# A fused Fourier filter and MLP on one core: the second tile's layer-norm statistics move to ScalarE, the first fifth of W1 is loaded in half rows, the second fifth ahead of x2, and the order is written anew

## The chip, the core and the metric

The kernel runs on one core of a Trainium2 chip. The metric is the device time of a run in microseconds (us). A core has five engines that run side by side, each with its own in-order list of instructions: TensorE (PE; its weight loads are listed as PEld), VectorE (DVE), ScalarE (ACT), GpSimd (POOL) and the sync engine (SP), which here issues most of the DMAs. They meet only at semaphores. A tile in this text is one of 16 groups of 128 rows of x; x0 and x1 are the loads of the first two, x2 is the load of tiles 2 and 3 together.

## The reference

The input x has 2048 rows of 640. Its normalized form goes through two branches, which are added to x:

```python
xn = _layernorm(x, axis=-1)                       # (x - mean) / sqrt(var + 1e-5)
X  = rfft2(xn, axes=(-2, -1)) * (w_r + 1j * w_i)  # branch A: a filter in the Fourier domain
a  = irfft2(X, s=(2048, 640)).astype(bfloat16)
h  = gelu(xn @ w1 + b1)                           # branch B: 640 -> 1536 -> 640
return x + a + (h @ w2 + b2)
```

x, the weights and the result are bfloat16.

## The kernel before

**The stages.** The 16 tiles are normalized (mean and variance over 640 columns, reciprocal root, then subtract and multiply). The normalized tile is needed in two forms: transposed, in `xnT`, for the first MLP product, and as it is, for the Fourier stages. Tiles 0 to 3 are transposed by TensorE against an identity into PSUM and copied out; tiles 4 to 15 are transposed by DMA. The Fourier branch folds the columns of each pair of tiles (lines 722 and 726), transforms over rows with a table (`gtab`), over columns (`etab`), mixes the rest (`mtab`), multiplies by the filter (line 837), and goes back by `ntab`, a DMA transpose, `getab` and `htab`. The MLP multiplies `W1` with `xnT`, applies the Gelu with the bias (line 770) into `gT`, and multiplies `gT` with `W2`. The last stage adds everything and stores it (lines 948 and 951).

**The head.** For each tile VectorE takes two `bn_stats` (line 666) over 320 columns and one `bn_aggr` (668). A third, constant set of statistics is arranged so that the aggregate's variance already holds the 1e-5. GpSimd then raises the variance to the power -0.5 (670), and VectorE subtracts and multiplies (691). Tile 0 is normalized in two pieces, 256 and 384 columns, so that its first two transposes can start early. The five 128-column blocks of tiles 0 and 1 are transposed in two lots, two and three (710), and copied out by ScalarE and VectorE (716).

**The first product.** `W1` comes in five loads, one for each 128 rows of its 640 (the fifths); each is 128 partitions by 1536 columns. The first block of the product (tiles 0 and 1, `BLOCKS[0]`) makes 12 groups of 128 outputs, and for the first two fifths treats tile 0 and tile 1 apart (128-column products, 48 of them), for the other three together (256 columns). Line 592 writes these loads, line 585 those of x.

**What sets the order.** All engines' lists are written out by hand as numbers in `ORDER` (line 158); a number is the place at which the operation was recorded. The class `Sched` lays these lists out with a model of costs, which chooses PSUM slots and the semaphore waits; it doesn't change the order of a list. On the sync queue x0, x1, the first fifth, x2, the second, third, fifth and fourth fifths go first, then more of x, the table `gtab`, and the rest. A product waits only for the fifth of `W1` that it reads. 38 products on zeros (`idle`, line 571) run on TensorE before there is data.

**Activation tables.** ScalarE evaluates its functions from a table set. A load instruction brings a set in; the kernel places one at the head for the Gelu (line 595), whose set serves the copies too. Where a function isn't in the set that is loaded, the build places a load right ahead of it.

Of the kernel before, what the change touches and what calls it, by code (L numbers as in the profile page):

```python
# [8 lines left out]
F32 = dt.float32  # L9
ACT = mybir.ActivationFunctionType  # L10
# [3 lines left out]
D = 640  # L14
# [109 lines left out]
class Pool:  # L124
# [34 lines left out]
    "sp": """8 13 14 17 15 16 19 18 21 22 20 27 30 23 26 28 153 155 166 168 32 31 35 46 48 37 179 181 192 194 38 39  # L159
41 34 44 33 29 52 49 40 205 219 221 207 43 42 50 45 51 47 36 54 508 506 505 507 529 531 530 532 554 553 53 555  # L160
556 578 577 580 579 597 642 606 623 633 669 659 678 741 695 750 732 715 766 705 775 782 789""",
    "pe": """7 117 55 119 278 260 122 233 251 242 124 269 234 270 243 252 261 281 254 236 235 279 253 263 272 245 264 273 237 282 275 138
# [8 lines left out]
713 776 777 764 770 778 771 779 772 773 780 783 784 785 786 787""",  # L171
    "act": """12 9 118 56 123 139 258 142 276 259 277 267 250 268 249 292 319 240 241 295 135 313 134 136 322 316 310 307 151 298 301 289
# [3 lines left out]
767 670 609 645 644 680 681 717 753""",  # L176
    "dve": """0 58 57 59 61 62 63 115 116 121 120 66 65 125 67 70 69 137 71 127 126 140 128 130 131 129 144 143 74 76 73 77
# [6 lines left out]
781 788""",  # L184
    "pool": """10 11 3 1 2 60 5 64 6 68 72 79 86 93 4 100 107 25 114 24 589 687 615 625 651 707 661 697 724 743 635 599
759 734 768 671""",
}

# [19 lines left out]
ROW_NS = {256: 26, 384: 22, 512: 27, 640: 33, 642: 70, 768: 37, 1024: 47, 1280: 56, 1600: 68, 2560: 103, 3072: 122, 4096: 160, 10272: 750, "acc": 152}  # L208
# [7 lines left out]
class Sched:  # L216
# [38 lines left out]
    def schedule(self):  # L255
# [31 lines left out]
        while left:  # L287
# [178 lines left out]
def bass_parallel_sum__spectral_gfnet__dense_activation_gelu__prompt_kernel(  # L466
# [21 lines left out]
    with ExitStack() as es:  # L488
        def sb(name, shape, dtype=BF):
            return es.enter_context(nc.sbuf_tensor(name, shape, dtype))  # L490
# [23 lines left out]
        rstd = sb("rstd", [128, 16], F32)  # L514
        W1 = sb("W1", [128, 5 * F])
# [49 lines left out]
        K.op([("pool", 0.1)], 94, lambda e, _: e.memset(stats[:, :, 14:15], D * 1e-5), writes=[B_eps])  # L565
        K.op([("pool", 0.1)], 100, lambda e, _: e.memset(mhalf[:], -0.5), writes=[B_mh])
# [12 lines left out]
        B_w1s = [Buf(f"w1_{j}") for j in range(5)]  # L579
        B_g, B_e, B_m, B_n, B_ge, B_h, B_w2 = [Buf(x) for x in ("g", "e", "m", "n", "i", "h", "w2")]  # L580
# [14 lines left out]
        K.op([("act", 1.3)], 420, lambda e, _: e.preload_act_table(ACT.Gelu_apprx_tanh), writes=[Buf("table")])  # L595
# [63 lines left out]
        mv_ops, st_op = [], {}  # L659
        for c0, n in [(c, 1) for c in range(4)] + [(c, 2) for c in range(4, 16, 2)]:  # L660
            pr = 100 - c0 / 2
            B_mv, B_r = Buf(f"mv{c0}"), Buf(f"r{c0}")
            for c in range(c0, c0 + n):
                B_st = Buf(f"st{c}")
                for h in range(2):
                    st_op[c] = K.op([("dve", 0.393)], pr, lambda e, _, c=c, h=h: e.bn_stats(stats[:, c, 6 * h:6 * h + 6], view(X, c * D + H2 * h, [[1, H2]])),  # L666
                         reads=[B_x[c]], writes=[B_st], gate=mv_ops[:1])
                mv_ops.append(K.op([("dve", 0.119)], pr, lambda e, _, c=c: e.bn_aggr(mv[:, c, :], stats[:, c, :]), reads=[B_st, B_eps], writes=[B_mv]))  # L668
            a, b = c0, c0 + n
            K.op([("pool", 0.65)], 500, lambda e, _, a=a, b=b: e.tensor_tensor(out=rstd[:, a:b], in0=mv[:, a:b, 1], in1=mhalf[:, a:b], op=ALU.pow),  # L670
                 reads=[B_mv, B_mh], writes=[B_r] + B_rs[a:b])

        for pair in range(8):
# [10 lines left out]
            for n in range(2):  # L684
# [3 lines left out]
                cuts = (0, 256, D) if not c else (0, D)  # L688
                B_xs = [Buf(f"xn_{c}") for _ in cuts[2:]] + [B_xn]
                for d0, d1, bx in zip(cuts, cuts[1:], B_xs):  # L690
                    o = K.op([("dve", 0.066 + (d1 - d0) / 1980.0)], pr, lambda e, _, c=c, n=n, xnv=xnv, d0=d0, d1=d1: e.tensor_scalar(  # L691
                        out=xnv(n, d0, [[1, d1 - d0]]), in0=view(X, c * D + d0, [[1, d1 - d0]]), scalar1=mv[:, c, 0:1], scalar2=rstd[:, c:c + 1], op0=ALU.subtract, op1=ALU.mult),
                        reads=[B_x[c], B_rs[c]], writes=[xn, bx])
                    norm_ops.append(o)
                if not c:
                    st_op[1].gate += [o] * G1
# [7 lines left out]
                for j0, j1, engs in ((0, 2, ["act"]), (2, 5, ["dve"])) if c < 2 else ((0, 5, ["dve", "act"]),):  # L704
# [8 lines left out]
                    if not c + j0:  # L713
                        tp.deps.remove(norm_ops[1])
# [30 lines left out]
        for bi, (c0, nt) in enumerate(BLOCKS):  # L745
            for fc in range(NFC):
# [4 lines left out]
                if bi:  # L751
                    hps, at, part_ = Buf(f"hps{c0}_{fc}", psum, 1, ZONE["hps"]), 0, []
                    for js in ((0, 1, 2), (3, 4)):
                        part_ = [pe([("128", len(js) * mm_us(128 * nt))], pr + 0.01 * len(part_), lambda c0=c0, nt=nt, fc=fc, hps=hps, js=js: [
                            (psb(hps.slot, [[1, 128 * nt]]), view(W1, F * j + 128 * fc, [[1, 128]]), xnT[:, c0:c0 + nt, j, :], j == 0, j == 4) for j in js],
                            reads=B_w1s + B_xnT[c0:c0 + nt], writes=[hps], gate=part_)]
                        l1_ops += part_
                        l1_of.setdefault(bi, []).extend(part_)
                else:
                    at = 256 * (fc % 2)  # L760
                    if not at:
                        hps, part_ = Buf(f"hps0_{fc}", psum, 1, ANY), []
                        for j in range(5):
                            for t0, t1 in ((0, 1), (1, 2)) if j < LONE else ((0, 2),):
                                part_.append(pe([("128", 2 * mm_us(128 * (t1 - t0)))], pr + 8 - j - 2 * t0, lambda fc=fc, hps=hps, j=j, t0=t0, t1=t1: [
                                    (psb(hps.slot, [[1, 128 * (t1 - t0)]], 256 * h + 128 * t0), view(W1, F * j + 128 * (fc + h), [[1, 128]]), xnT[:, t0:t1, j, :], j == t0 == h == 0, j == 4) for h in range(2)],
                                    reads=[B_w1s[j]] + [B_xnL[t][j] for t in range(t0, t1)], writes=[hps], gate=part_[:1]))
# [37 lines left out]
        for P in range(4):  # L805
# [28 lines left out]
            for pair, Y, TB, Z in zip(two, Ys, TBs, Zs):  # L834
# [5 lines left out]
                for r, op in enumerate((ALU.subtract, ALU.add)):  # L840
                    K.op([("dve", dve_us(2 * KP, 2))], pr, lambda e, _, TB=TB, Z=Z, r=r, op=op: e.tensor_tensor(
                        out=view(Zb, Z.slot * 4 * KP + r * KP, [[2 * KP, 2], [1, KP]]), in0=tv(TB, 0, r), in1=tv(TB, 1, r), op=op), reads=[TB], writes=[Z])
# [32 lines left out]
        for gi, (c0, n) in enumerate(GROUPS):  # L875
# [20 lines left out]
            for i in range(n):  # L896
# [9 lines left out]
                else:  # L906
                    ki = [b for b in range(16) if b not in HOME].index(c)
                    free = norm_ops[:2 * ki + 3]
# [82 lines left out]
```

## Time and profile before

| | |
|---|---|
| median of 3 runs | 148.41 us (148.24 to 148.72) |
| span of the profiled execution, first to last instruction | 146.2 us |
| profiled execution's own time | not given beside its span; 2.2 us lie between that span and the median |
| TensorE, VectorE, ScalarE, GpSimd busy | 140.4, 110.9, 81.1, 23.7 us |
| granted TensorE clock | 1.000 |
| HBM read, written | 13.54 MB, 2.62 MB |

A line of the profile gives start, length, engine, source line, operation, the tiles it writes and reads, and in brackets the time the engine stood idle before it and what released it. Groups give the busy time, the mean of one in ns, and the idle time before them. L546 is the helper through which all products are recorded, L557 and L558 the copies by ScalarE and VectorE, L541 the loads; there one goes by the tiles. W stands for `W1` and `W2`, T for the buffer that holds the normalized tiles.

### The profile page before, as it was taken

Reading aid. Unit: us, or ns where it says so; the run is one execution under the profiler, and the core shown is the slowest. Engines: PE = TensorE matmul, PEld = TensorE weight load, DVE = VectorE, ACT = ScalarE, POOL = GpSimd, SP = SyncE. Lnnn points to the kernel's source line nnn. Section 1 sums busy time; section 2 is a strip of 40 time slices with the busy share of each in tenths; the row PEclk is TensorE's granted clock in tenths of the full one; section 3 lists DMA queues with packets and bytes.
Section 4 is the critical chain, followed back from the end, with each engine's and each line's share of the span. In section 5 each row is a group of like instructions: output and inputs, shape, how many; then the busy total and the mean of one; then the engine's idle time right before and its main releaser. Section 6 shows DMA issues by size and latency. Waiting matters only on the chain.

```text
span 146.2 us, 4076 instructions
## 1 busy us (share of the span) xinstructions
PE 140.4 (96%) x1702; PEld 91.3 (62%) x1720; DVE 110.9 (76%) x233; ACT 81.1 (55%) x145; POOL 23.7 (16%) x40
## 2 busy tenths in 40 slices
PE   7999999999999999999999999999999999999993
PEld 7788998988455464457554645554446766556572
DVE  1799999999953459799877967982203998998982
ACT  3208999999989769763555633225476655201000
POOL 2330401304200009220200040000063700000000
DMA  4999998998999676968446844462569885103234
GB/s 105 328 394 354 319 164 197 203 175 229 241 238 160 162 195 137 242 126 167 89 92 128 56 95 89 46 142 56 91 129 225 178 188 180 45 4 137 90 135 135
DMA packets 30842, 23.63 MB, mean 162 GB/s; under 512 B 20457, under 2 KB 26857, under 8 KB 30697
## 3 DMA queue, kind: packets, MB, share of 16 engines
q1 hardware_dynamic: 28432, 17.81, 52.6%
q0 software_dynamic: 2368, 5.57, 17.6%
q8 instruction: 13, 0.21, 0.6%
q14 instruction: 5, 0.03, 0.1%
q10 hardware_dynamic: 24, 0.00, 0.0%
HBM read 13.54 MB, written 2.62 MB: 111 GB/s over the span
## 4 chain that ended last, share of the span: by engine, by line
PE 92%; DMA 4%; issue 1%; SPq 1%; DVE 0%
PE ps L546 91%; DMA W<-in_B_w_dram 4%; SPq L541 1%; PE ps L710 0%; DVE W L948 0%
## 5 line engine op out<-in xcount | busy, mean ns | idle before, releaser
L546 PE MATMUL ps<-xnT,W 128*128 128x256 bf16 (+2 forms) x384 | 58.8, 300 | 0.2
L546 PE MATMUL ps<-W,gT 128*128 128x512 bf16 (+3 forms) x380 | 55.7, 292 | 1.6 <-issue 1.1
L546 PEld LDWEIGHTS ps<-W,gT 128*128 128x128 bf16 x396 | 30.3, 98 | 23.4 <-issue 1.9
L546 PEld LDWEIGHTS ps<-xnT,W 128*128 128x128 bf16 x384 | 33.3, 98 | 16.4 <-issue 1.7
L770 ACT ACTIVATE gT<-ps,b1col 128x256 bf16<-128x256 f32 (+1 forms) x72 | 35.3, 558 | 6.8 <-PE ps L546 6.5
L666 DVE BATCH_NORM_STATS2 stats<-X 128x6 f32<-128x320 bf16 x32 | 13.9, 475 | 2.9 <-DMA X<-in_A_x_dram 2.9
L557 ACT ACTIVATE Wf<-ps 128x960 bf16<-128x960 f32 (+1 forms) x8 | 7.0, 902 | 13.7 <-PE ps L546 13.7
L933 POOL DMA_DIRECT2D X<-in_A_x_dram x8 | 7.1, 1132 | 40.5 <-DMA Wf<-in_A_w_r_dram 17.2
L837 DVE TENSOR_TENSOR T<-Y,Wf 128x1288 bf16<-128x1288 bf16 x16 | 12.7, 825 | 0.1
L670 POOL TENSOR_TENSOR rstd<-mv,mhalf 128x2 f32<-128x2 f32 (+1 forms) x10 | 7.2, 717 | 27.5 <-DVE mv L668 27.3
L557 ACT ACTIVATE Xb<-ps 128x960 bf16<-128x960 f32 (+1 forms) x7 | 7.7, 1106 | 6.7 <-PE ps L546 6.7
L933 POOL DMA_DIRECT2D xnT<-in_A_x_dram x8 | 7.5, 1154 | 24.2 <-ACT xnT L915 24.2
L558 DVE CAST Y<-ps 128x644 bf16<-128x644 f32 x8 | 6.5, 827 | 5.4 <-PE ps L546 5.4
L557 ACT ACTIVATE XV<-ps 128x1280 bf16<-128x1280 f32 (+3 forms) x10 | 9.5, 963 | 0.7 <-PE ps L546 0.7
L558 DVE CAST Wf<-ps 128x640 bf16<-128x640 f32 (+1 forms) x4 | 4.0, 990 | 7.6 <-PE ps L546 7.6
L558 DVE CAST Xb<-ps 128x960 bf16<-128x960 f32 (+1 forms) x5 | 5.9, 1178 | 4.1 <-PE ps L546 4.0
L726 DVE TENSOR_TENSOR T<-T 128x512 bf16<-128x512 bf16 (+1 forms) x32 | 8.5, 311 | 0.0
L691 DVE TENSOR_SCALAR T<-X,mv,rstd 128x640 bf16<-128x640 bf16 (+2 forms) x17 | 7.1, 430 | 0.9 <-POOL rstd L670 0.7
L546 PE MATMUL ps<-getab,XV 32*128 32x160 bf16 (+1 forms) x128 | 7.5, 241 | 0.0
L948 DVE TENSOR_TENSOR W<-ps,X 128x640 bf16<-128x640 f32 x8 | 6.5, 822 | 1.1 <-PE ps L546 1.1
L546 PEld LDWEIGHTS ps<-getab,XV 32*128 32x128 bf16 (+1 forms) x128 | 6.5, 146 | 1.3
L887 DVE TENSOR_TENSOR Wf<-Wf 128x960 bf16<-128x960 bf16 (+1 forms) x12 | 7.0, 597 | 0.4 <-ACT Wf L557 0.3
(52 smaller groups left out, 133.4 us busy)
## 6 DMA issues: line engine op xcount, KB each, us to landing
X<-in_A_x_dram POOLq DMA_DIRECT2D x8, 320.0 KB, 4.3
xnT<-in_A_x_dram POOLq DMA_DIRECT2D x8, 320.0 KB, 5.2
out_dram<-W SPq DMA_DIRECT2D x15, 160.0 KB, 1.8
X<-in_A_x_dram SPq DMA_DIRECT2D x7, 320.0 KB, 7.0
W<-in_B_w_dram SPq DMA_DIRECT2D x5, 384.0 KB, 5.9
W<-in_B_w_dram SPq DMA_DIRECT2D x4, 480.0 KB, 7.8
Wf<-in_A_w_i_dram SPq DMA_DIRECT2D x6, 160.5 KB, 5.4
Wf<-in_A_w_r_dram SPq DMA_DIRECT2D x6, 160.5 KB, 4.8
```

The source lines that it names most:

```text
L546: ins = e.matmul(o_, lhsT=lw, rhs=rh, start=st, stop=sp_, skip_group_check=True)
L557: return e.activation(dst(), src(), ACT.Copy, scale=scale)
L558: return e.tensor_copy(dst(), src())
L666: st_op[c] = K.op([("dve", 0.393)], pr, lambda e, _, c=c, h=h: e.bn_stats(stats[:, c, 6 * h:6 * h + 6], view(X, c * D + H2 * h, [[1, H2]]) ...
L670: K.op([("pool", 0.65)], 500, lambda e, _, a=a, b=b: e.tensor_tensor(out=rstd[:, a:b], in0=mv[:, a:b, 1], in1=mhalf[:, a:b], op=ALU.pow), ...
L691: o = K.op([("dve", 0.066 + (d1 - d0) / 1980.0)], pr, lambda e, _, c=c, n=n, xnv=xnv, d0=d0, d1=d1: e.tensor_scalar(out=xnv(n, d0, [[1, d1 ...
L726: ring_ops.append(K.op([("dve", dve_us(4 * w, 2))], pr, lambda e, _, op=op, x1v=x1v, xfv=xfv, o_=o_, o0=o0, o1=o1, w=w: e.tensor_tensor(ou ...
L770: K.op([("act", act_us(128 * nt, 1))], pr + PRIO["gelu"] + GP[bi], lambda e, _, c0=c0, nt=nt, fc=fc, hps=hps, at=at: e.activation(gT[:, fc ...
L837: filt_ops.append(K.op([("dve", dve_us(4 * KP, 2))], pr, lambda e, _, k=k, Y=Y, TB=TB, pair=pair: e.tensor_tensor(out=view(TT, TB.slot * 8 ...
L887: K.op([("dve", dve_us(320 * n, 2))], pr + 2, lambda e, _, k=k, op=op, yo=yo, y2=y2, n=n: e.tensor_tensor(out=view(Wf, Y2 + y2.slot * 3 * ...
L933: xo_ops[c] = K.op([("pool", 0.9)], 51 - c / 20, lambda e, _, c=c, xov=xov: e.dma_start(xov(0, D), xv[:, c, :], accum_op=ALU.add), reads=[ ...
L948: K.op([("dve", dve_us(w))], 95, lambda e, _, os_=os_, fps=fps, o0=o0, w=w, xov=xov, base=base: e.tensor_tensor(out=view(W1, OST + os_.slo ...
```

## The change

1. The statistics of tile 1 are no longer VectorE's. ScalarE runs a Copy over the tile with scale -1/640, whose accumulated output is minus the mean, and a Square with that as bias, whose accumulated output is the sum of squared deviations. The elementwise results go into the buffer `Z`, which is not in use then, and the first writers of `Z` are made to wait for them.
2. The roots of tiles 0 and 1 are taken by ScalarE (Sqrt, for tile 1 with scale 1/640 and a bias of 1e-5 from a new constant) and inverted by VectorE; GpSimd's power stays for tiles 2 to 15. A preload of the Sqrt set is recorded beside that of the Gelu set.
3. Tile 1 is normalized in two pieces as tile 0 is, with an addition in place of the subtraction. The first copies of tile 0 out of PSUM go to VectorE in place of ScalarE.
4. The first fifth of `W1` is loaded in two halves of 768 columns, each with its own semaphore.
5. `ORDER` is new throughout, and two tables, `LAND` and `LATE`, tell the planner's model when loads land. On the sync queue the second fifth now goes ahead of x2. On TensorE, 20 wide products of the first block stand ahead of the transposes of tile 2, where there were 10.

```diff
 ORDER = {
-    "sp": """8 13 14 17 15 16 19 18 21 22 20 27 30 23 26 28 153 155 ...
+    "sp": """9 15 16 17 18 20 19 22 21 24 25 23 30 33 26 29 31 158 160 ...
-    "act": """12 9 118 56 123 139 258 142 276 ...
+    "act": """14 65 63 66 67 59 128 11 282 281 ...
...
+LAND = {9: 3.13, 15: 3.63, 16: 4.9, 17: 5.6, 18: 6.7, 19: 8.5, 20: 7.5, ...
-                o.end = done + TAIL + lag(t, size)
+                o.end = max(t + 2.0, LAND[o.seq]) if o.seq in LAND else done + TAIL + lag(t, size) + LATE.get(o.seq, 0.0)
...
+        epsc = sb("epsc", [128, 1], F32)
+        K.op([("pool", 0.1)], 94, lambda e, _: e.memset(epsc[:], 1e-5), writes=[B_eps])
+        B_w1z = Buf("w1_0z")
...
         def load_w1(j, q="sp"):
-            load(view(W1, F * j, [[1, F]]), w1v[:, j, :], B_w1s[j], (8, 2 * F), q=q)
+            halves = ((0, F // 2, B_w1s[0]), (F // 2, F, B_w1z)) if not j else ((0, F, B_w1s[j]),)
+            for f0, f1, b in halves:
+                load(view(W1, F * j + f0, [[1, f1 - f0]]), w1v[:, j, f0:f1], b, (8, 2 * (f1 - f0)), q=q)
...
+        K.op([("act", 1.3)], 420, lambda e, _: e.preload_act_table(ACT.Sqrt), writes=[Buf("table")])
-        K.op([("act", 1.3)], 420, lambda e, _: e.preload_act_table(ACT.Gelu_apprx_tanh), writes=[Buf("table")])
+        K.op([("act", 1.3)], 420, lambda e, _: e.preload_act_table(ACT.Gelu_apprx_tanh), writes=[Buf("table2")])
...
+                if c == 1:
+                    for k, (f, kw) in enumerate(((ACT.Copy, dict(scale=-1.0 / D)), (ACT.Square, dict(bias=mv[:, 1, 0:1])))):
+                        act_st.append(K.op([("act", act_us(D))], pr, lambda e, _, k=k, f=f, kw=kw: e.activation(
+                            Zb[:].bitcast(F32)[:, 0:D], view(X, D, [[1, D]]), f, accum_out=mv[:, 1, k:k + 1], **kw),
+                            reads=[B_x[1]] + [B_st] * k, writes=[B_mv if k else B_st]))
+                    continue
...
+            if a < 2:
+                B_sd = Buf(f"sd{a}")
+                K.op([("act", 0.19)], 500, lambda e, _, a=a: e.activation(rstd[:, a:a + 1], mv[:, a, 1:2], ACT.Sqrt, bias=epsc[:] if a else 0.0, scale=1.0 / D if a else 1.0),
+                     reads=[B_mv, B_eps], writes=[B_sd])
+                K.op([("dve", 0.08)], 500, lambda e, _, a=a: e.reciprocal(rstd[:, a:a + 1], rstd[:, a:a + 1]), reads=[B_sd], writes=[B_rs[a]])
+                continue
...
-                cuts = (0, 256, D) if not c else (0, D)
+                cuts = (0, 256, D) if c < 2 else (0, D)
...
-                for j0, j1, engs in ((0, 2, ["act"]), (2, 5, ["dve"])) if c < 2 else ((0, 5, ["dve", "act"]),):
+                for j0, j1, engs in ((0, 2, ["act"] if c else ["dve"]), (2, 5, ["dve"])) if c < 2 else ((0, 5, ["dve", "act"]),):
```

In the numbers of the changed ScalarE list, 14 is the b1 load, 65 and 66 are the Copy and the Square, 63 and 67 the roots of tiles 0 and 1, 59 is b1col, 128 the evacuation of tile 1, 11 the preload of the Gelu set. Number 10, the preload of the Sqrt set, stands in the later part of the list (`... 701 639 10 529 530 711 532 444 ...`), where 529, 530 and 532 are evacuations of the inverse transform and 444 is a Gelu.

More of the change, by code (lines that the diff above doesn't have):

```diff
@@ new lines @@
+585 584 602 647 611 628 638 674 664 683 746 700 755 737 720 771 710 780 787 794""",
+    "pe": """8 121 123 58 256 238 127 265 274 129 240 283 247 276 275 249 241 266 250 248 286 239 257 284 267 259 251 269 278
[9 rows of a table added]
+776 781 708 782 777 778 788 783 784 785 789 790 791 792""",
+    "act": """14 65 63 66 67 59 128 11 282 281 147 255 245 272 254 273 324 263 246 264 321 294 318 297 139 141 140 306 300 327
[3 rows of a table added]
+563 566 553 556 738 578 580 468 459 453 471 747 465 456 587 462 613 763 649 650 772 675 685 686 723 722 757""",
+    "dve": """0 61 60 62 64 119 120 68 122 125 126 124 131 130 132 69 70 74 71 73 136 75 134 135 142 145 133 144 80 77 78 81 79
[6 rows of a table added]
@@ new lines @@
+699 745 760 754 759 762 736 719 761 770 709 779 786 793""",
+    "pool": """12 13 4 1 2 3 6 7 72 76 83 90 97 5 104 111 28 118 27 594 692 620 630 656 712 666 702 729 748 640 604 764 739 773
+676""",
+}
+LAND = {9: 3.13, 15: 3.63, 16: 4.9, 17: 5.6, 18: 6.7, 19: 8.5, 20: 7.5, 21: 10.5, 22: 9.5, 23: 14.89, 24: 11.84, 25: 12.65, 26: 17.41, 29: 18.61, 30: 15.54, 31: 19.46, 33: 16.42}
+LATE = {27: 0.4, 28: 0.7, 32: 2.0, 34: 1.0, 36: 0.5, 37: 1.6, 38: 1.4, 40: 1.4, 41: 0.4, 42: 1.7, 43: 2.3, 44: 1.7, 45: 0.2, 46: 0.4, 47: 2.5, 48: 0.4, 49: 2.2, 50: 0.9, 51: 1.6, 52: 2.9, 53: 0.3, 54: 1.2, 55: 2.5, 160: 0.3, 173: 0.9, 184: 1.0, 186: 1.0, 197: 0.6, 210: 1.0, 224: 0.7, 594: 1.1}
@@ L691, in bass_parallel_sum__spectral_gfnet__dense_activation_gelu__prompt_kernel @@
                     o = K.op([("dve", 0.066 + (d1 - d0) / 1980.0)], pr, lambda e, _, c=c, n=n, xnv=xnv, d0=d0, d1=d1: e.tensor_scalar(
-                        out=xnv(n, d0, [[1, d1 - d0]]), in0=view(X, c * D + d0, [[1, d1 - d0]]), scalar1=mv[:, c, 0:1], scalar2=rstd[:, c:c + 1], op0=ALU.subtract, op1=ALU.mult),
+                        out=xnv(n, d0, [[1, d1 - d0]]), in0=view(X, c * D + d0, [[1, d1 - d0]]), scalar1=mv[:, c, 0:1], scalar2=rstd[:, c:c + 1], op0=ALU.add if c == 1 else ALU.subtract, op1=ALU.mult),
                         reads=[B_x[c], B_rs[c]], writes=[xn, bx])
@@ L712, in bass_parallel_sum__spectral_gfnet__dense_activation_gelu__prompt_kernel @@
                     tp = K.op([("pe", nj * mm_us(128))], pr, xt, reads=[B_xs[0] if j0 == 0 else B_xn, xn, B_id], writes=[tps], alts=[[("128", nj * mm_us(128))]])
-                    if not c + j0:
-                        tp.deps.remove(norm_ops[1])
+                    if c < 2 and not j0:
+                        tp.deps.remove(norm_ops[2 * c + 1])
                     us = {"dve": 0.06 + 0.07 * nj, "act": act_us(128 * nj)}
@@ L755, in bass_parallel_sum__spectral_gfnet__dense_activation_gelu__prompt_kernel @@
                             (psb(hps.slot, [[1, 128 * nt]]), view(W1, F * j + 128 * fc, [[1, 128]]), xnT[:, c0:c0 + nt, j, :], j == 0, j == 4) for j in js],
-                            reads=B_w1s + B_xnT[c0:c0 + nt], writes=[hps], gate=part_)]
+                            reads=B_w1s + [B_w1z] + B_xnT[c0:c0 + nt], writes=[hps], gate=part_)]
                         l1_ops += part_
@@ L766, in bass_parallel_sum__spectral_gfnet__dense_activation_gelu__prompt_kernel @@
                                     (psb(hps.slot, [[1, 128 * (t1 - t0)]], 256 * h + 128 * t0), view(W1, F * j + 128 * (fc + h), [[1, 128]]), xnT[:, t0:t1, j, :], j == t0 == h == 0, j == 4) for h in range(2)],
-                                    reads=[B_w1s[j]] + [B_xnL[t][j] for t in range(t0, t1)], writes=[hps], gate=part_[:1]))
+                                    reads=[B_w1z if not j and fc >= NFC // 2 else B_w1s[j]] + [B_xnL[t][j] for t in range(t0, t1)], writes=[hps], gate=part_[:1]))
                         l1_ops += part_
@@ L841, in bass_parallel_sum__spectral_gfnet__dense_activation_gelu__prompt_kernel @@
                     K.op([("dve", dve_us(2 * KP, 2))], pr, lambda e, _, TB=TB, Z=Z, r=r, op=op: e.tensor_tensor(
-                        out=view(Zb, Z.slot * 4 * KP + r * KP, [[2 * KP, 2], [1, KP]]), in0=tv(TB, 0, r), in1=tv(TB, 1, r), op=op), reads=[TB], writes=[Z])
+                        out=view(Zb, Z.slot * 4 * KP + r * KP, [[2 * KP, 2], [1, KP]]), in0=tv(TB, 0, r), in1=tv(TB, 1, r), op=op), reads=[TB], writes=[Z], after=act_st)
             B_us = [Buf(f"u{pair}") for pair in two]
@@ L907, in bass_parallel_sum__spectral_gfnet__dense_activation_gelu__prompt_kernel @@
                     ki = [b for b in range(16) if b not in HOME].index(c)
-                    free = norm_ops[:2 * ki + 3]
+                    free = norm_ops[:2 * ki + 4]
                     def xov(o0, w, ki=ki):
```

19 lines of the change are left out of this document (5 added, 14 removed), and 35 rows, old and new, of the table ORDER.

## The prediction

> **What bounds the kernel now.** I read the page's span and engine lines first, then the chain that ended last, then the first 12 us instruction by instruction, engine by engine, because the edit acts there. The first fence holds the engine line and pieces of the chain in order of time (start, length, what); its span is 146.2 us.
>
> ```profile
> PE 140.4 (96%) x1702; PEld 91.3 (62%) x1720; DVE 110.9 (76%) x233; ACT 81.1 (55%) x145; POOL 23.7 (16%) x40
> ...
> 2.68 5.39 DMA W<-in_B_w_dram
> 8.08 0.05 issue
> 8.12 2.35 PE ps L546 x28
> ...
> 12.16 38.28 PE ps L546 x390
> ...
> 143.74 0.33 DVE W L948
> ```
>
> From 8.12 us to 143.74 us the chain is TensorE alone, broken only by short issue pieces. TensorE's order is written out, so whatever delays its work in the head moves the end by the same amount, and whatever engines beside it save later is worth nothing. The question is how much TensorE work is done by which time. The head, TensorE and its weight loads (the bracket is the idle time before, and its releaser):
>
> ```profile
> 1.06 4.23 PE L546 MATMUL ps<-warm 128*128 128x128 bf16 x38 [1.06 <-DVE warm L562]
> 5.55 0.30 PE L710 MATMUL ps<-ident,T 128*128 128x128 bf16 x2 [0.26 <-DVE T L691]
> 6.32 0.40 PE L546 MATMUL ps<-xnT,W 128*128 128x128 bf16 x4
> 6.57 0.27 PE L710 MATMUL ps<-ident,T 128*128 128x128 bf16 x2
> 6.67 0.50 PE L546 MATMUL ps<-xnT,W 128*128 128x128 bf16 x6
> 7.18 3.29 PE L546 MATMUL ps<-xnT,W 128*128 128x128 bf16 x40
> 10.31 0.44 PE L710 MATMUL ps<-ident,T 128*128 128x128 bf16 x5
> 7.12 0.75 PEld L546 LDWEIGHTS ps<-xnT,W 128*128 128x128 bf16 x12
> 8.12 1.16 PEld L546 LDWEIGHTS ps<-xnT,W 128*128 128x128 bf16 x20 [0.25 <-DMA W<-in_B_w_dram]
> ```
>
> The weight loads show the one stop inside the head: after 4 + 6 + 12 = 22 products of 128 columns, TensorE stands for 0.25 us until the second fifth of W1 lands. Of the x40 group, 28 products follow: 18 of 128 columns (half units) and 10 of 256 (units), 19 units in 8.12 to 10.31, so 0.115 us for 256 columns and 0.058 for 128. The mark I compare at is "ten transposes of tiles 0 and 1 and forty 128-column products done": before, 8.12 + 18 x 0.058 = 9.16. The changed order does the same fifty things before its first 256-column product, too. What feeds them:
>
> ```profile
> 0.81 0.88 SPq L541 DMA_DIRECT2D X<-in_A_x_dram  x2
> 3.15 0.89 DVE L666 BATCH_NORM_STATS2 stats<-X 128x6 f32<-128x320 bf16 x2 [2.15 <-DMA X<-in_A_x_dram]
> 4.07 0.22 DVE L668 BATCH_NORM_AGGREGATE mv<-stats 128x2 f32<-128x15 f32 x1
> 4.21 0.82 DVE L666 BATCH_NORM_STATS2 stats<-X 128x6 f32<-128x320 bf16 x2
> 4.38 0.58 POOL L670 TENSOR_TENSOR rstd<-mv,mhalf 128x1 f32<-128x1 f32 x1 [2.82 <-DVE mv L668]
> 5.21 0.57 DVE L691 TENSOR_SCALAR T<-X,mv,rstd 128x256 bf16<-128x256 bf16 x2
> 7.19 0.89 DVE L666 BATCH_NORM_STATS2 stats<-X 128x6 f32<-128x320 bf16 x2 [0.51 <-DMA X<-in_A_x_dram]
> 1.45 1.28 ACT L595 ACT_TABLE_LOAD   x1 [1.45 <-PEq L976]
> 5.88 0.39 ACT L557 ACTIVATE xnT<-ps 128x256 bf16<-128x256 bf16 x1 [3.15 <-PE ps L710]
> ```
>
> Here the reader sees tile 0's path (statistics, mean and variance, GpSimd's power, normalization, transposes at 5.55), and that ScalarE has one table load, wholly inside its idle time.
>
> **The change, part by part.** The order of the changed program holds what the diff doesn't say outright. The explicit Sqrt preload is not at the head of ScalarE's list: it stands far back, ahead of an inverse-transform evacuation. ScalarE's list therefore begins with the b1 DMA, a load of a default set, the Copy on tile 1, a load of the Sqrt set, the root of tile 0, the Square on tile 1, the root of tile 1, b1col, the evacuation of tile 1's first two blocks, the Gelu load, then the Gelus. Three loads in the head in place of one, and two more later (the preload and a return to Gelu). Only the second is exposed: it can't start before tile 1's Copy has gone, and tile 0's root waits for it. These rows give the durations:
>
> ```profile
> L915 ACT ACTIVATE X<-b2bc 128x640 f32<-128x640 bf16 x8 | 5.8, 743 | 0.0
> L652 ACT ACTIVATE b1col<-ps 128x12 f32<-128x12 f32 x1 | 0.2, 174 | 0.0
> L562 DVE MEMSET warm<- 128x64 uint32 x1 | 0.1, 112 | 0.9 <-PEq L976 0.9
> L558 DVE COPY xnT<-ps 128x384 bf16<-128x384 bf16 x2 | 0.7, 346 | 0.0
> L691 DVE TENSOR_SCALAR T<-X,mv,rstd 128x256 bf16<-128x256 bf16 x1 | 0.3, 285 | 0.0
> L770 ACT ACTIVATE gT<-ps,b1col 128x256 bf16<-128x256 f32 x48 | 19.7, 489 | 2.6 <-PE ps L546 2.3
> ```
>
> Handovers between engines are 0.09 (the aggregate ends at 4.29, GpSimd starts at 4.38) or 0.05 (first normalization ends 5.21 + 0.285 = 5.50, transpose 5.55).
>
> *Tile 0.* x0 was issued at 0.81 and used at 3.15; x1, issued 0.44 later and at the same queue place after the change, lands near 3.6 (an estimate from that; the trace bounds it by 3.15 and 4.21, where VectorE took it up without waiting). Copy 3.65 + 0.74 = 4.39 (row of the same shape). Reading out an accumulator is in no row: zero below, the shortest ScalarE row, 0.17, above; I take the middle, 0.09, since nothing is nearer: 4.48. Sqrt load 1.28: 5.76. Root (row of b1col, 0.17): 5.93. Handover, reciprocal (shortest VectorE row, 0.11): 6.13. Normalization from 6.20 to 6.49, its second part to 6.77. First transposes 6.54 against 5.55, so 0.99 later; of that the load is 1.28, and the two roots' way without GpSimd's 0.58 gives some back.
>
> *Tile 1.* Square 5.93 + 0.74 + 0.09 = 6.76, root 6.93, reciprocal 7.02 to 7.13. VectorE's order puts this reciprocal ahead of tile 0's first evacuation (which the change moves from ScalarE to VectorE), so that copy, though its transposes are done at about 6.8, waits behind it: 7.13 + 0.3 (from the 0.346 of 384 columns) = 7.43, first product 7.50 against 6.32. Normalization 7.40 to 7.70, its transposes 7.75 against 6.57, ScalarE's evacuation 8.08 to 8.47 (0.33 after the transposes' start, as 5.55 to 5.88 before), second part's transposes ready at 8.03.
>
> *TensorE.* 4 products 7.50 to 7.73, two transposes to 7.87, 4 products to 8.10, three transposes to 8.27, 8 products to 8.73, then 24 products that need tile 1 (ready 8.52) to 10.12. Against 9.16: **0.96 us later**.
>
> *W1.* The second fifth goes ahead of x2. Landings before were x2 at 7.19 and this fifth at 8.08, 384 KB in 0.9 us. Ahead of 320 KB of x2, it lands about 0.8 earlier, 7.3; it is needed at 8.15. The 0.25 us wait goes, but TensorE is later than the data, so nothing is gained. What is late next is x2, about 8.1: VectorE takes it up only at about 9.4, behind tile 0 and 1's folds. Two half loads put one more issue (0.43) ahead of everything behind on the sync queue; the later fifths land, at 384 KB per 0.9 to 1.0 us, at 9.0, 10.0 and 10.9, needed at 10.1, 11.3 and 12.2. Zero, under that cover of 0.9 to 1.3; without the delay it would be gone. The queue then stands until the transposes (the first row is for the next part):
>
> ```profile
> 10.86 1.02 DVE L726 TENSOR_TENSOR T<-T 128x512 bf16<-128x512 bf16 x4
> 9.00 0.52 SPq L541 DMA_DIRECT2D X<-in_A_x_dram  x1
> 15.94 5.32 SPq L698 DMA_TRANSPOSE xnT<-T  x4
> ```
>
> *Tiles 2 and 3.* From 9.4 VectorE has four statistics, two aggregates and three folds: 0.41 x 4 + 0.14 x 2 (starts 4.07 and 4.21) + 0.8 (three of the four in the row above) = 2.7, then normalizations to 12.6 and 13.0. TensorE, with 20 wide and 4 narrow products put in front (20 x 0.115 + 0.23), asks at 12.65 and 12.95. Zero, no more than 0.1.
>
> *The rest.* VectorE's statistics of tile 1 (0.82 + 0.22) leave, GpSimd loses two powers and gains a memset: beside other work, zero. What queues on ScalarE behind the Copy's wait for x1 is all of the above, with b1col, which comes at about 7 and isn't needed before the first Gelu. The Gelu load (8.47 to 9.75) precedes the first Gelu, which came at 11.92 before; zero. The two late loads, 2.57 together, fall among evacuations where ScalarE stood idle before them:
>
> ```profile
> 11.92 0.48 ACT L770 ACTIVATE gT<-ps,b1col 128x256 bf16<-128x256 f32 x1 [0.43 <-PE ps L546]
> 85.35 0.77 ACT L557 ACTIVATE U<-ps 128x512 bf16<-128x512 f32 x2 [2.03 <-PE ps L546]
> 88.19 0.47 ACT L770 ACTIVATE gT<-ps,b1col 128x256 bf16<-128x256 f32 x1 [1.50 <-PE ps L546]
> 80.00:100.00 20.00, 19.58 (x291) 10.62 (x292) 16.12 (x27) 7.88 (x16) 1.78 (x2) 1.00 0.59 92
> ```
>
> With 7.88 us of ScalarE work in 20 I take zero, and 2.57 as the other end. The new order elsewhere can't gain: the changed program issues as many matmuls of each shape, and there is no stop but issue to remove. It can lose.
>
> **Sum.** 146.2 + 0.96 = 147.2 of span; 2.2 us lie between the profiled span and the median 148.41, and stay. 148.41 + 0.96 = 149.37, so 149.4. With x1 at 3.15 and free accumulators the delay is 0.96 - 0.45 - 0.17 = 0.34 (148.75); with x1 at 4.21, reads at 0.17 and 0.1 for a pointer bias in two steps (the Gelu's 489 ns against 0.39 us for a Copy of as many columns) 0.96 + 0.61 + 0.16 + 0.2 = 1.93 (150.3).
>
> **Rivals.** *The Sqrt load hides (not slower).* If it ran during the wait for x1, or cost tile 0 nothing, everything above would be 1.28 earlier where TensorE is ready: first product 6.2, mark about 8.75, a gain of up to 0.4. But then the W1 fifths (9.0, 10.0, 10.9) become last by about 0.1 to 0.3, so 148.1. It decides from a load costing tile 0 less than 0.3. Against it: an in-order list in which the load stands behind an instruction that waits for x1, and a row of 1.28 us.
>
> *A pause behind the load.* The load's row ends at 2.73 and ScalarE's next work is at 5.88, so a pause of up to 3.15 behind it wouldn't have shown. A pause as long as the load itself (1.28) delays both roots: 150.7. The Trainium skill, "ScalarE: Activation LUTs", section "What ACT_TABLE_LOAD costs", says that a switch of sets takes 1283 ns for the load and about 1380 ns for a drain; by that an estimate of 150.8. The trace agrees on the first figure (1.28 us), and no run here shows the second.
>
> *The late loads or the new order stop TensorE.* Were half of the 2.57 exposed, 150.7; the idle rows above speak against it.
>
> **How the numbers follow.** 0.3% is 0.45 us, about what a measurement of this kernel can tell from no change. The forecast, 148.75 to 150.3: 0.66. Pause: 0.14. Late stops: 0.07. Hidden load: 0.13. Likeliest 149.4. I cut the range at 148.5, leaving out the hidden load, and at 150.9, just above the pause. Slower holds nearly all of the first three cases, less a corner of the forecast below 148.86: 0.82; the hidden load and that corner give 0.12 within 0.3% and 0.06 faster.
>
> **What would show it.** Right: three table loads before 10 us, one of them between tile 1's Copy and the first root; first transposes near 6.5, first product near 7.5, 128-column products done near 10.1; no wait for W1; TensorE without stops after that. Wrong: transposes before 6 (the load hid), after 7.3 (a pause), or TensorE idle between 75 and 95 us behind ScalarE.

## The result and the profile after

The changed kernel takes 152.9 us (median of four runs, 152.54 to 153.34) against 148.56 (148.24 to 148.79) for the kernel before on the same chip: a ratio of 1.029, with an interval of 1.027 to 1.032. It is slower, as predicted, but by 4.3 us where 0.96 was predicted, and outside the range. The profiled execution took 152.54 us, its span is 150.4 us, 4.2 more than before. Runs of one kernel differ here by when TensorE's pace rises or falls in the head, so where it matters the text gives the runs singly.

From the page of the changed kernel: the engines, and the granted TensorE clock in 40 slices of 3.76 us (a digit is tenths of full speed, 9 is 90% or more).

```profile
PE 142.1 (94%) x1701; PEld 92.8 (62%) x1720; DVE 106.8 (71%) x231; ACT 91.4 (61%) x157; POOL 22.7 (15%) x39
...
PEclk9959999999999999999999999999999999999999
```

TensorE is busy 1.7 us longer with as much work, and the third slice, 7.5 to 11.3 us, ran at about half the clock. The head of the changed kernel, instruction by instruction (start, length, engine, line, tiles, idle time before and its releaser):

```profile
3.62 0.74 ACT L678 ACTIVATE Z<-X 128x640 f32<-128x640 bf16 x1 [0.88 <-DMA X<-in_A_x_dram]
4.26 0.19 ACT L678 ACTIVATION_READ_ACCUMULATOR Z<-X 128x1 f32 x1
4.47 1.28 ACT L689 ACT_TABLE_LOAD   x1
5.76 0.20 ACT L689 ACTIVATE rstd<-mv 128x1 f32<-128x1 f32 x1
...
6.81 0.29 ACT L689 ACTIVATE rstd<-mv,epsc 128x1 f32<-128x1 f32 x1
...
6.00 0.16 DVE L691 RECIPROCAL rstd<-rstd 128x1 f32<-128x1 f32 x1 [1.71 <-ACT rstd L689]
...
1.06 3.80 PE L552 MATMUL ps<-warm 128*128 128x128 bf16 x38 [1.06 <-DVE warm L568]
6.60 0.63 PE L733 MATMUL ps<-ident,T 128*128 128x128 bf16 x5 [1.74 <-DVE T L714]
...
7.54 0.53 PE L552 MATMUL ps<-xnT,W 128*128 128x128 bf16 x4 [0.21 <-DVE xnT L564]
...
8.83 5.43 PE L552 MATMUL ps<-xnT,W 128*128 128x128 bf16 x56
14.10 0.72 PE L733 MATMUL ps<-ident,T 128*128 128x128 bf16 x10
```

The chain to the first product came within 0.06 us of what was predicted: load done at 5.75 (5.76 predicted), first transposes at 6.60 (6.54), first product at 7.54 (7.50). No wait for W1 is left. But after the zeros, which end at 4.86, TensorE stands for 1.74 us, and then 56 products, 36 of them narrow (128 columns) and 20 wide (256), take 5.43 us. The same stretch in windows of 1 us (window, length, PE busy and matmuls, granted clock, DMA share, GB/s):

```profile
5.00:6.00 1.00, 0.00 (x0) 1.00 0.88 321
6.00:7.00 1.00, 0.40 (x4) 1.00 1.05 330
7.00:8.00 1.00, 0.79 (x10) 0.83 0.86 276
8.00:9.00 1.00, 1.00 (x12) 0.50 0.97 366
9.00:10.00 1.00, 1.00 (x12) 0.50 1.02 387
10.00:11.00 1.00, 1.00 (x12) 0.50 1.03 409
11.00:12.00 1.00, 1.00 (x17) 0.96 1.04 414
```

By the 0.83 and the 0.96 the clock is at half from 7.66 to 11.08 us. The missing parts of the last five windows add up to 0.17 + 3 x 0.50 + 0.04 = 1.71 us of clock. The record begins at 1.00, but TensorE doesn't begin at full pace: the weight loads of the zeros take 148 ns each until 4.2 us and 100 from 4.3, those of the first product 151 from 8.2 to 10 us and 98 from 11.3.

Further on there are stops that before did not have. What TensorE waited for (total, times, longest), in the kernel before (the last line is the head, and ahead of the zeros both kernels stand for 1.1):

```profile
PE ps L546 <- issue: 1.3, 8, 0.2
...
PE ps L710 <- DVE T L691: 0.3, 1, 0.3
```

And in the changed kernel, the head's 1.7 first:

```profile
PE ps L733 <- DVE T L714: 1.7, 1, 1.7
...
PE ps L552 <- DVE X L962: 1.0, 1, 1.0
...
PE ps L552 <- DMA XV<-U: 0.4, 1, 0.4
...
PE ps L552 <- DVE Wf L915: 0.2, 1, 0.2
```

The longest of the three later ones, in the chain of the changed kernel (start, length, what); the other two stand at 114.7 (0.4) and between 122 and 130 us (0.2):

```profile
60.56 1.30 ACT Y L563 x2
61.86 0.63 ACT X L938
...
62.78 1.11 POOL X L956 x2
63.90 7.33 DMA X<-in_A_x_dram
...
71.25 0.82 DVE X L962
...
74.56 0.75 DVE X L962
...
75.57 0.43 PE ps L552 x2
```

Line 938 copies the second bias into the buffer of one tile, line 956 is GpSimd's DMA that adds x to it, line 962 is VectorE's addition that frees a PSUM slot. GpSimd's queue, before first, then after (the second copy for that queue begins on ScalarE only at 61.74, behind two evacuations):

```profile
54.78 3.63 POOL L933 DMA_DIRECT2D X<-in_A_x_dram  x4 [17.18 <-DMA Wf<-in_A_w_r_dram]
```

```profile
56.59 0.93 POOL L956 DMA_DIRECT2D X<-in_A_x_dram  x1 [16.80 <-DMA Wf<-in_A_w_r_dram]
62.78 3.57 POOL L956 DMA_DIRECT2D X<-in_A_x_dram  x4 [5.27 <-ACT X L938]
```

Before, four of these DMAs went out at once. In the changed order the second copy (number 691 in ScalarE's list) stands behind more work, so GpSimd's queue stands for 5.27 us with three more DMAs behind it. The late one takes 7.33 us to land, VectorE waits for it at the head of its own list, and TensorE 1.04 us for VectorE.

So the 4.2 us are: the late head, 0.84; the half clock, about 1.6; the three later stops, 1.04 + 0.4 + 0.2 = 1.64. That is 4.1. The first two are split with the experiment c2 below. The rest is not assigned, and neither are the short stops listed as issue, 1.3 before and 0.5 after.

### The profile page after: what moved, and what is told of

It is laid out like the page before. It is cut to its first block, busy times and chain, and to the rows that moved or that the text cites. A ratio compares the mean times of both kernels' runs of the same rounds, so it can differ in the third digit from the quotient of the medians.

```text
span 150.4 us, 4083 instructions
## 1 busy us (share of the span) xinstructions
PE 142.1 (94%) x1701; PEld 92.8 (62%) x1720; DVE 106.8 (71%) x231; ACT 91.4 (61%) x157; POOL 22.7 (15%) x39
## 4 chain that ended last, share of the span: by engine, by line
PE 75%; DMA 9%; ACT 5%; SPq 3%; DVE 3%; issue 2%; POOL 1%
PE ps L552 75%; DMA X<-in_A_x_dram 6%; SPq L885 3%; DMA XV<-U 2%; ACT Y L563 1%; ACT Z L678 1%; DVE X L962 1%; DVE Z L864 1%; ACT L689 1%; POOL X L956 1%; PE ps L733 1%; ACT gT L793 1%; ACT T L563 1%; DVE T L860 0%; ACT X L938 0%
## 5 line engine op out<-in xcount | busy, mean ns | idle before, releaser
L552 PE MATMUL ps<-W,gT 128*128 128x128 bf16 (+3 forms) x379 | 55.3, 291 | 2.2 <-DVE X L962 1.0
L552 PEld LDWEIGHTS ps<-xnT,W 128*128 128x128 bf16 x384 | 35.0, 101 | 15.5 <-issue 1.9
L563 ACT ACTIVATE Wf<-ps 128x960 bf16<-128x960 f32 (+1 forms) x9 | 7.9, 910 | 7.5 <-PE ps L552 7.5
L563 ACT ACTIVATE Xb<-ps 128x960 bf16<-128x960 f32 (+1 forms) x8 | 9.0, 1166 | 4.2 <-PE ps L552 4.2
L563 ACT ACTIVATE U<-ps 128x512 bf16<-128x512 f32 (+1 forms) x12 | 4.6, 434 | 8.8 <-PE ps L552 4.6
L564 DVE CAST Wf<-ps 128x640 bf16<-128x640 f32 (+1 forms) x3 | 2.8, 936 | 9.4 <-PE ps L552 9.4
L563 ACT ACTIVATE Y<-ps 128x644 bf16<-128x644 f32 x9 | 6.2, 706 | 5.1 <-PE ps L552 5.1
L971 DVE TENSOR_TENSOR W<-ps,xnT 128x640 bf16<-128x640 f32 (+2 forms) x10 | 6.9, 690 | 2.8 <-PE ps L552 2.5
L749 DVE TENSOR_TENSOR T<-T 128x128 bf16<-128x128 bf16 (+1 forms) x32 | 8.5, 308 | 0.1
L962 DVE TENSOR_TENSOR X<-ps,X 128x640 f32<-128x640 f32 x8 | 6.6, 820 | 2.8 <-DMA X<-in_A_x_dram 1.6
```

The lines of the kernel that those rows point to most:

```text
L552: ins = e.matmul(o_, lhsT=lw, rhs=rh, start=st, stop=sp_, skip_group_check=True)
L563: return e.activation(dst(), src(), ACT.Copy, scale=scale)
L564: return e.tensor_copy(dst(), src())
L749: ring_ops.append(K.op([("dve", dve_us(4 * w, 2))], pr, lambda e, _, op=op, x1v=x1v, xfv=xfv, o_=o_, o0=o0, o1=o1, w=w: e.tensor_tensor(ou ...
L962: kept_ops.append(K.op([("dve", dve_us(D))], 30, lambda e, _, kps=kps, xov=xov: e.tensor_tensor(out=xov(0, D), in0=psb(kps.slot, [[1, D]]) ...
L971: K.op([("dve", dve_us(w))], 95, lambda e, _, os_=os_, fps=fps, o0=o0, w=w, xov=xov, base=base: e.tensor_tensor(out=view(W1, OST + os_.slo ...
```

## The experiments

**The clock, by more zeros.** Theory: the half clock comes from the 1.74 us in which TensorE had nothing. 64 zero products instead of 38 fill that time; the second argument, a cost for the planner, stays as it was.

```diff
-        idle(WARM[0], WARM[0] * 0.11)
+        idle(64, WARM[0] * 0.11)
```

> The changed kernel with 64 products on zeros at the start in place of 38, so that TensorE is busy until about 6.4 us, when the first transposes come. Theory 'clock': the granted clock of 0.50 between 8 and 11 us comes from TensorE standing idle between the zeros (end 4.85) and the first transposes (6.59); without the idle stretch the clock stays at 1.00, and about 1.6 us come back: 151.3 us. Rival 'the half clock costs nothing, or doesn't come from the idle stretch': 152.9, with the clock at 0.50 again.

151.42 us (150.6 to 151.65), ratio 1.019 (1.015 to 1.022), from 1.029: 1.5 us came back, as the theory said (151.3). The row of the zeros ends at 7.27 and overlaps the first transposes, which came at 7.10 instead of 6.60, and still tile 2's transposes began at 12.72 instead of 14.10. The slow pace was a cost by itself. TensorE's waits in this run:

```profile
PE ps L552 <- DVE X L962: 0.6, 1, 0.6
PE ps L552 <- ACT gT L793: 0.6, 1, 0.6
```

The stop behind VectorE is still there. The second one is new: at 24.2 us TensorE waits for ScalarE's Gelus.

**The Sqrt load at the head.** The prediction's rival of the hidden load: with the load out of the way the head is earlier, and W1 becomes last.

```diff
-    "act": """14 65 63 66 67 59 128 11 ...  701 639 10 529 ...
+    "act": """14 10 65 63 66 67 59 128 11 ... 701 639 529 ...
```

> The changed kernel with the preload of the Sqrt set moved from its late place to the head of ScalarE's list, so that one load in ScalarE's idle time serves the Copy, the Square and the roots, and the two late loads go as well. Theory 'exposed load and clock': first transposes at 5.3 us, first product at 6.25, the clock at 1.00, so 1.28 for the load and 1.6 for the clock come back: 150.0 us if the waits between 60 and 115 us belong to the new order, 148.3 if they came from the late loads or from the late head. Rival 'the load hides elsewhere': 152.5.

151.7 us (150.42 to 152.82), ratio 1.024 (1.019 to 1.030). The transposes came at 5.15 and the first product at 6.12, and then W1 was last, as that rival said (0.1 to 0.3 was its price; it was 0.50 and 0.19). The profiled run:

```profile
7.55 1.96 PE L552 MATMUL ps<-xnT,W 128*128 128x128 bf16 x32 [0.50 <-DMA W<-in_B_w_dram]
```

```profile
PE ps L552 <- DMA XV<-U: 1.4, 1, 1.4
PE ps L552 <- DMA W<-in_B_w_dram: 0.7, 2, 0.5
```

Neither 150.0 nor 148.3 came. A head 1.4 us earlier did not make a fast kernel: W1 took back 0.7, and a later wait, for the last DMA transpose of the inverse stage, took 1.4.

**Without the late loads.** The preload of Sqrt far back brings two table loads near 80 us. The preload is left out; the three loads of the head stay.

```diff
-        K.op([("act", 1.3)], 420, lambda e, _: e.preload_act_table(ACT.Sqrt), writes=[Buf("table")])
+        K.op([("act", 1.3)], 420, lambda e, _: None, writes=[Buf("table")])
```

> The changed kernel without the explicit Sqrt preload (the build still puts its load ahead of the first root), so that the two late loads near 80 and 84 us are gone and the head is as it was. Theory 'late loads hidden': 152.9 us within 0.3, head and waits as before. Rival 'late loads make the waits between 60 and 115 us': down by up to 1.7, 151.2.

The time says nothing: 151.40 and 150.29 us in two runs (ratio 1.016 by these), 154.94 and 154.95 in two others, with a mean clock of 0.978. The trace does say something. The two longer stops stand nearly as they were, so the late loads do not make them (the one of 0.2 is not in this trace, but a2, which has no late loads either, has it at 0.3):

```profile
PE ps L552 <- DVE X L962: 0.8, 1, 0.8
PE ps L552 <- DMA XV<-U: 0.4, 1, 0.4
```

It also shows the head of the changed kernel in a run whose recorded clock is 1.00 throughout:

```profile
9.00:10.00 1.00, 1.00 (x12) 1.00 1.03 399
10.00:11.00 1.00, 1.00 (x19) 1.00 1.04 405
```

Twelve products in the window to 10 us is the half pace of the changed kernel, and the weight loads from 8.2 to 10 us take 147 ns; those of the zeros take 149. So in this run the pace had not risen before the gap and did not rise until about 10 us, and the record does not show it. Tile 2's transposes begin at 13.70 us, 0.40 earlier than in the changed kernel's trace.

**The old order behind the head.** The lists of before on all engines behind the head, the Sqrt load at the head.

```diff
-    "pe": """8 121 123 58 256 238 127 265 274 ...
+    "pe": """8 121 58 123 283 265 127 238 256 ...
...
-    "act": """14 65 63 66 67 59 128 11 282 281 ...
+    "act": """14 10 65 63 66 67 59 128 11 144 263 ...
```

> The changed kernel with the Sqrt preload at the head of ScalarE's list and, from tile 2 on, the old order of all engines (the sync queue keeps the second fifth of W1 ahead of x2, and the half loads). Theory 'new order makes the waits': no wait of TensorE over 0.2 us between 60 and 115 us, 148.2 us, about 1.7 less than the same with the new order. Rival 'the waits come from elsewhere': as long as with the new order, 150.0.

160.18 us, ratio 1.079 (1.076 to 1.081). This doesn't decide between the two. The planner gave the products other PSUM banks with this list (the eight slots into which TensorE writes), and TensorE waited for evacuations that before it did not wait for:

```profile
PE ps L528 <- ACT gT L769: 5.2, 8, 1.1
```

**The same with the banks of before written out,** and x2 ahead of the second fifth again.

```diff
-    "sp": """9 15 16 17 18 20 19 ...
+    "sp": """9 15 16 17 20 18 19 ...
...
+        psum.pins = iter("001206006000000042517346767567655444576674456765676476777566465457776667...")
```

> The changed statistics of tile 1 and roots on ScalarE with the Sqrt preload at the head, and the half loads, but behind that head the order of the kernel before on every engine (x2 ahead of the second fifth of W1 too) and its PSUM banks, written out. Theory 'the new order makes the waits between 60 and 115 us': none of them is there, first transposes at 5.3, 148.3 us within 0.4. Rival 'the statistics on ScalarE cost something later by themselves': 149.5 or more, with waits in the middle.

149.12 us (ten runs, 148.99 to 150.23), ratio 1.0045 (1.001 to 1.008), which neither the theory (148.3 within 0.4) nor the rival (149.5 or more) had. Its waits behind the zeros:

```profile
PE ps L534 <- DVE mv L667: 0.4, 1, 0.4
PE ps L534 <- DMA W<-in_B_w_dram: 0.4, 1, 0.4
```

Both lie in the head (at 8.43 for W1, at 9.99 for tile 2's statistics). None of the later stops of the changed kernel is there, so they belong to the new order together with the banks that the planner gave it, not to the statistics on ScalarE; this run doesn't part order from banks. And a head that is 0.38 us earlier than before (first transposes at 5.17 against 5.55) gives nothing: W1 (8.43 against 8.12 before) and tile 2 then come last.

**The delay alone.** The kernel before with two unused powers on GpSimd ahead of tile 0's root (the lists renumbered).

```diff
+            if not a:
+                for k in range(2):
+                    K.op([("pool", 0.0)], 500, lambda e, _, k=k: e.tensor_tensor(out=junk[:, k:k + 1], in0=mv[:, 0:1, 1], in1=mhalf[:, 0:1], op=ALU.pow), ...
```

> The kernel before with two more powers of 128x1 on GpSimd ahead of tile 0's root, their results unused: tile 0's and tile 1's roots come about 1.1 us later, and nothing else changes. Theory 'a late head costs its length, and the clock on top': first transposes at 6.65, TensorE idle for 1.4 us after the zeros, then products at half rate for some us: 151.0 us. Rival 'the length alone': 149.4, all products of the head at 0.058 us.

150.23 us (ten runs, 148.8 to 150.38), ratio 1.009 (1.005 to 1.013): 1.85 us for a head that is 0.91 later (first transposes at 6.46 against 5.55). First transposes, and one window, of the profiled run:

```profile
6.46 0.40 PE L714 MATMUL ps<-ident,T 128*128 128x128 bf16 x2 [1.16 <-DVE T L695]
```

```profile
9.00:10.00 1.00, 1.00 (x12) 1.00 1.01 393
10.00:11.00 1.00, 1.00 (x19) 1.00 1.04 416
```

Twelve products in the window to 10 us and nineteen in the next, at a recorded clock of 1.00 in both, as in a3: here the pace of the products is the safer reading, since twelve is what the changed kernel did at 0.50. So in the kernel before, too, a delay costs more than its own length: 1.85 - 0.91 = 0.94 us, and somewhat more for the pace, as this run no longer waits 0.25 us for W1.

**The second fifth ahead of x2 alone,** in the kernel before.

```diff
-    "sp": """8 13 14 17 15 16 19 ...
+    "sp": """8 13 14 15 17 16 19 ...
```

> The kernel before with the second fifth of W1 ahead of x2 on the sync queue, nothing else. Theory 'nothing to gain': the wait of 0.25 us for that fifth goes, but tiles 2 and 3 land 0.9 later and TensorE waits for their transposes: 148.8 us (148.3 to 149.2). Rival 'it gains the wait': 148.0.

148.45 us (ten runs, 147.92 to 149.37), ratio 0.999 (0.996 to 1.003). The wait for W1 is gone, tile 2 is not waited for in its place, and no gain can be measured. The half loads are not tried alone in any run.

**ScalarE's copy earlier.** Number 691 is the copy of the bias behind which GpSimd's queue stood. It moves up in ScalarE's list; the zeros are the 64 of a1.

```diff
-    ... 237 236 417 655 476 402 ... 441 515 516 691 728 509 ...
+    ... 237 236 417 655 691 476 402 ... 441 515 516 728 509 ...
-        idle(WARM[0], WARM[0] * 0.11)
+        idle(64, WARM[0] * 0.11)
```

> The changed kernel with 64 products on zeros (as in the run with the long warm-up, 151.42 us) and one of ScalarE's copies of b2 (for tile 8) moved ahead by 20 places, from behind two evacuations near 61 us to about 45 us. Theory 'GpSimd's adding DMAs are late because they queue behind that copy, and VectorE waits for one of them': GpSimd issues the first of these DMAs without the gap of 5 us, VectorE's wait near 71 us goes, and TensorE's 0.6 us behind it: 150.8 us. Rival 'the DMAs are late by themselves': 151.4, the wait stays.

149.83 us (149.51 to 151.73), ratio 1.011 (1.000 to 1.022), 1.6 below a1 by the medians. GpSimd's queue in this run:

```profile
55.78 4.53 POOL L956 DMA_DIRECT2D X<-in_A_x_dram  x5 [17.44 <-DMA Wf<-in_A_w_r_dram]
```

Five DMAs go at once, and VectorE's wait and TensorE's 0.6 us behind it are gone. The 1.6 us can't all be put down to the copy: a1's stop of 0.6 us at 24.2 is gone from this trace as well, and it stands ahead of the place to which the copy moved (about 46 us). Why is open.

**The copy alone,** with the 38 zeros of the changed kernel (the first two lines of the diff above).

> The changed kernel with the copy of b2 for tile 8 moved ahead by 20 places on ScalarE, nothing else. Theory 'three terms that add up: late head 1.0, clock 1.6, this copy 1.6': GpSimd's gap and VectorE's wait near 71 us go, 151.3 us; the head and its clock stay as they were. Rival 'the copy only mattered together with the long warm-up': 152.9.

150.63 us as median, the four runs 149.73, 150.21, 151.05 and 152.98; ratio 1.011 (1.006 to 1.017) without the last. The profiled run is that last one:

```profile
8.00:9.00 1.00, 1.00 (x12) 0.50 0.96 336
```

```profile
PE ps L552 <- DMA XV<-U: 1.9, 1, 1.9
```

The stop behind VectorE is gone, and in its place the wait for the last DMA transpose is 1.9 instead of 0.4. With one stop taken away, that one is next: in this run the last transpose took 4.77 us to land, in the changed kernel 3.55. The two fastest runs have a mean recorded clock of 1.0, with the same head. That does not show that they kept the full pace: a3's traced run has it too.

**Without the late loads, with a steady clock and the early copy.** b4 without the Sqrt preload.

```diff
-        idle(WARM[0], WARM[0] * 0.11)
+        idle(64, WARM[0] * 0.11)
...
-        K.op([("act", 1.3)], 420, lambda e, _: e.preload_act_table(ACT.Sqrt), writes=[Buf("table")])
+        K.op([("act", 1.3)], 420, lambda e, _: None, writes=[Buf("table")])
```

> The changed kernel with 64 products on zeros, the copy for tile 8 moved ahead (as in the run that gave 149.83 us) and without the explicit Sqrt preload, so without the two late table loads. Theory 'late loads hidden': 149.8 us within 0.3. Rival 'they cost': 148.5 or less.

150.14 us (149.71 to 150.56), ratio 1.010 (1.006 to 1.014). That is b4's time within its spread, and nothing near the rival's 148.5: the late loads cost nothing that can be seen. This run also gives the head at full pace:

```profile
7.57 0.40 PE L552 MATMUL ps<-xnT,W 128*128 128x128 bf16 x4 [0.20 <-DVE xnT L564]
...
8.34 4.36 PE L552 MATMUL ps<-xnT,W 128*128 128x128 bf16 x56
12.53 0.72 PE L733 MATMUL ps<-ident,T 128*128 128x128 bf16 x10
```

With the first product at 7.57, as in the changed kernel, tile 2's transposes begin at 12.53 and not at 14.10: 1.57 us is the price of the half clock. Ahead of that place stand 44 narrow and 20 wide products. From the prediction's mark, forty narrow ones done at 9.16, the kernel before would reach it four narrow and 20 wide products later, at 9.16 + 0.23 + 20 x 0.115 = 11.69. So the late head is 0.84 without the clock.

**All three mended:** 42 zeros, the Sqrt load at the head, the early copy.

```diff
-    "act": """14 65 63 66 67 59 128 11 ... 237 236 417 655 476 ...
+    "act": """14 10 65 63 66 67 59 128 11 ... 237 236 417 655 691 476 ...
...
-        idle(WARM[0], WARM[0] * 0.11)
+        idle(42, WARM[0] * 0.11)
```

> The changed kernel with the Sqrt preload at the head, the copy for tile 8 moved ahead and 42 products on zeros: exposed load, clock and late copy all mended. Theory 'the three terms are all there is, and what is then last is W1': first transposes at 5.3 to 5.5 us, waits for W1 of 0.5 to 0.7 us in the head, no wait over 0.3 after it, 148.8 us (148.3 to 149.3). Rival 'the statistics on ScalarE then gain': 148.0 or less, faster than the kernel before.

150.15 us (149.46 to 150.9), ratio 1.010 (1.005 to 1.015). The first product comes at 6.29, and then:

```profile
7.77 4.53 PE L552 MATMUL ps<-xnT,W 128*128 128x128 bf16 x56 [0.55 <-DMA W<-in_B_w_dram]
...
23.82 2.34 PE L552 MATMUL ps<-xnT,W 128*128 128x256 bf16 x20 [0.77 <-ACT gT L793]
```

The theory (148.8) missed a wait: W1 takes back 0.55 as it said, but at 23.8 ScalarE's Gelus come last for 0.77. From there on TensorE is no earlier than in c2 (23.82 against 23.59), so the head's gain is spent before 25 us. No version with ScalarE's statistics beat the kernel before.

**The pace in all thirteen traces.** In four TensorE stands idle for 1.16 us or more between the zeros and the first transposes (b2 1.16, a3 1.29, c1 1.63, the changed kernel 1.74). In these the weight loads of the first product take 147 to 151 ns from 8.2 to 10 us. In the other nine it stands for 0.76 us at most, and they take 97 or 98 ns from 7.2 us on.

## Why the prediction was wrong

**The failed step is the sum.** It took the late head, 0.96, for the whole effect, where 4.3 us were measured. That term was nearly right (0.84 in c2), and two others stood at nothing: the pace of TensorE behind the gap, and the new order.

*The pace behind the gap.* The prediction has no term and no rival for it. It moved the first transposes from 5.55 to 6.54 and kept 0.058 us for a narrow product after an idle time of well over 1 us. The row it quoted spoke of it: 38 zeros in 4.23 us are 0.111 each, twice 0.058, so TensorE's pace in the head was known to be no constant. Measured: half the pace for 3.4 us, which cost 1.57 us (against c2) and 1.5 (against a1); b2 shows the same in the kernel before, by a delay alone. The Trainium skill, "TensorE: Matmul & The Clock Gate", section "Why this matters for your kernels", advises against idle gaps above about 3 us; here 1.74 us were followed by the half clock, and 1.16 us (b2) by the slow pace, so the measurement decides. How long the gap must be (0.76 us did no harm in b3), what of the time around it counts, and why the pace had risen before it in some traces (the changed kernel) and not in others (a3), stays open.

*The new order.* "The new order elsewhere can't gain" was followed by "It can lose", but the loss was put at zero, with a chance of 0.07 for late loads or order together. That as many matmuls of each shape are issued says nothing of the queues beside TensorE. The step that was left out is to read GpSimd's list with what each of its DMAs waits for: one copy placed late on ScalarE held it for 5.27 us. The stop behind it was 1.04, and it goes when that copy moves (b4, c1); 0.6 lie in two other stops, which b1 lays to the order and its banks but no run separates further. Why the last DMA transpose lands after 3.55 us in one run and 4.77 in another is open.

**What was right.** The order on ScalarE and the exposed load, 1.28, and the chain to the first transposes and the first product within 0.06; in it tile 1's root took 0.29 where 0.17 was taken. The estimate of 0.09 for reading an accumulator holds as what it adds: its row is 0.19 long, but it starts 0.10 before the Copy's end (3.62 + 0.74 = 4.36, 4.26). The second fifth of W1 ahead of x2 gains nothing (b3). The late loads are hidden (c2 against b4).

**The rivals.** No pause follows the load: it ends at 5.75 and the root starts at 5.76. The Trainium skill's drain of about 1380 ns ("ScalarE: Activation LUTs", section "What ACT_TABLE_LOAD costs") does not show here; of its two figures only the 1283 ns do. The hidden load was right about what would come last (W1 in a2 and c3), but not about a gain. "The late loads or the new order stop TensorE" was right about the order; its price was worked out from the late loads, which are hidden.

## What to carry to other kernels

When a change lets TensorE stand at the start, price the pace of what follows as well as the delay, and look in the trace for any stretch where the same product takes twice as long. When an order is written anew, read each list for the first instruction that waits on another engine and count what is queued behind it, GpSimd's DMAs included: equal work on the busiest engine says nothing of that. And when a first stop is taken away, ask which is next; here the filled gap brought 1.5 us (a1), the load at the head, which shortens the gap too, 1.2 (a2), and the early copy 1.6 on top of a1 (b4), but all three together brought 2.75 (c3).

## What the runs showed of the hardware

TensorE began at half pace in the traces: 0.111 us for each of the 38 zeros of the kernel before, and weight loads of 145 to 149 ns against 98 later. In the changed kernel the loads went to 100 ns at about 4.25 us, and the granted clock fell to 0.50 for 3.4 us after an idle time of 1.74 us and a busy share of 0.40 and 0.79 in the two windows of 1 us behind it. In a3 and b2 the pace stayed slow until about 10 us, at a recorded clock of 1.00 (twelve products in 1 us against nineteen), so the length of the weight loads is the safer sign. A table load took 1.28 us, and the next instruction began 0.01 us later. An accumulator is read by an instruction of its own, 0.19 us long, of which 0.09 lies behind the main one. GpSimd's adding DMAs of 320 KB took 6.1 us to land in the median of the changed kernel, 4.3 in the kernel before, and 7.33 where one was waited for.
